# Group 1 of an attention-then-MLP kernel: layer 2 by Strassen's seven block products, with its rows normalised on GpSimd

## The chip, the cores and the metric

The kernel runs on one core of one Trainium2 chip. The core has a matrix engine (TensorE; in the profile PE, and PEld for its weight loads), VectorE (DVE), ScalarE (ACT), GpSimd (POOL), and SyncE (SP), which here issues nearly all DMAs. The metric is device time of one execution, in microseconds; a kernel's time is the median of several executions. Ratios are the mean time of one kernel's fast runs over the mean time of the other's fast runs of the same rounds, so they are not quite the ratio of the medians quoted beside them.

## The reference

```python
# attention: q, k, v of shape (8, 8, 576, 64); causal, window of 64
scores = scale * q @ k.T, masked to 0 <= i - j < 64
attn   = softmax(scores) @ v
x      = attn.transpose(0, 2, 1, 3).reshape(8, 576, 512)
# MLP with a residual
xn  = (x - mean) / sqrt(var + 1e-6) * g_ln
out = x + maximum(xn @ w_ch1, 0) @ w_ch2     # 512 -> 2048 -> 512
```

## The kernel before

The rows are worked off in nine groups of 512: one for the first 512 rows of each of the eight batches, one for all the rest. In every period PE does the MLP of group g in "units" of about 0.87 us, and between the units, at numbered slots, attention steps of the next group are put in. `at(18, b_step, 1, 0)` means: after unit 18, do attention step `b_step` for block 0 of group 1. Where the traces of this case were compared with the program, an engine's instructions stood in its order (in the changed kernel the first z of group 1, whose statistics were ready at 44.3 us, ran on GpSimd at 52.59 us, behind the casts queued before it), so a slot number is read here as setting the order on all engines at once.

A block is 128 rows. `b_step` ends in the block's mean and variance (`mvg`). `z_step` makes the normalised block z, `zt_step` transposes it to zT, the input of layer 1:

```python
def z_step(g, kb):
    ...
    if g < 2:      # groups 0 and 1: VectorE subtracts the mean only, one instruction
        nc.vector.tensor_scalar(out=z, in0=xv, scalar1=mu, scalar2=None, op0=ALU.subtract)
        return
    # groups 2 and on: full normalisation, four dependent GpSimd instructions
    nc.gpsimd.tensor_scalar(out=ve, in0=var, ...)               # var + eps
    nc.gpsimd.tensor_tensor(out=rs, in0=ve, in1=mhalf, op=ALU.pow)
    nc.gpsimd.tensor_scalar(out=nm, in0=mu, scalar1=rs, ...)    # -mean * rs
    nc.gpsimd.tensor_scalar(out=z, in0=xv, scalar1=rs, scalar2=nm, ...)

def zt_step(g, kb, eng="act"):
    if XZ <= g < NGRP - 1 and not (kb == 3 and g in (3, 5)):    # XZ = 2
        nc.sync.dma_start_transpose(out=zT[g][...], in_=z)       # by DMA, SyncE's queue
        return
    ...                                                          # by PE, copied by ScalarE
```

In groups 0 and 1 the scale 1/sqrt(var) is computed later by Newton steps on VectorE and multiplied in after layer 2. Strassen's scheme adds and subtracts blocks of different rows before layer 2, so it needs rows that are fully normalised. Groups 2 and on use it: seven products of half the size in each direction, with four row sums (`s_sums`, VectorE, on the hidden tile hrT) and four sums of blocks of W2 (`w2_sums`, VectorE, once for all groups). Layer 2 of groups 0 and 1 is the plain product: 64 matmuls of 512 columns.

Before the loop over the groups, the program already queues casts on GpSimd, each of which waits for its load:

```python
cast_qk(1, 0); cast_v(1, 0, 1); cast_v(1, 1, 2)
for i in range(8):
    w2_cast(i)                       # W2, in eight pieces
    ...
load_qk(1, 1); load_v(1, 2, 4)
cast_qk(1, 1); cast_v(1, 2, 3); cast_v(1, 3, 4)
# ... here begins the loop over the groups with its slots
```

The softmax here doesn't subtract the row's maximum and nothing guards it: scores larger than these inputs give would overflow.

## Time and profile before

| | before |
|---|---|
| time, first 3 runs | 313.44 and 313.60 us (the third, 504.55, is a slow run and is not used) |
| profiled execution, span | 313.0 us (its time was 314.71 us, 1.2 us above the others) |
| PE busy | 298.9 us, 95% |
| granted TensorE clock, mean | 0.999 |
| group 1: layer 1, layer 2 begin at | 58.75 us, 78.94 us |
| group 2: layer 1 begins at | 96.43 us |

From the page of the kernel before: busy time of the engines, and the granted clock in 40 slices of the span (in tenths; 9 is 90% or more).

```profile
PE 298.9 (95%) x3041; PEld 194.1 (62%) x3041; DVE 205.2 (66%) x385; ACT 153.4 (49%) x258; POOL 166.3 (53%) x251
...
PEclk9999999999999999999999999999999999999999
```

PE is the engine that bounds the kernel (busy for 95% of the span). The timeline of PE around the first two z transposes of group 1 (start, duration, engine, line, operation; in brackets the idle time before and what ended it; xps rows left out):

```profile
46.30 0.39 PE L357 MATMUL ztp<-ident,z 128*128 128x128 f16 x4
47.75 1.46 PE L528 MATMUL ch<-w2s,hrT 128*128 128x512 f16 x6 [1.06 <-POOL w2s L201]
49.04 0.39 PE L357 MATMUL ztp<-ident,z 128*128 128x128 f16 x4
```

PE transposes the first z block at 46.30 us and the second at 49.04 us without waiting: VectorE had written them. The only wait here is for the cast of a piece of W2 (1.06 us). The timeline of GpSimd in the same stretch:

```profile
46.66 1.04 POOL L201 CAST w2s<-w2s 128x1024 f16<-128x1024 f32 x1 [1.27 <-DMA w2s<-in_moe_w_ch_dram]
48.27 1.04 POOL L128 CAST qk<-qk 128x1024 f16<-128x1024 f32 x1 [0.57 <-DMA qk<-in_q_dram]
49.94 1.04 POOL L128 CAST qk<-qk 128x1024 f16<-128x1024 f32 x1 [0.63 <-DMA qk<-in_k_dram]
50.92 1.17 POOL L147 CAST vA<-v 128x512 f16<-128x512 f32 x2
```

The last W2 cast ends at 47.7 us, and the casts of q, k and v of group 1 end at 52.1 us; they wait for their loads. Nobody needs GpSimd for a z of group 1.

Two pieces of the chain that ended last show what a plain and a Strassen matmul cost on PE (start, duration, what):

```profile
79.11 0.86 PE ch L404 x4
...
122.29 1.75 PE pA L464 x16
```

Four plain matmuls take 0.86 us, sixteen of a Strassen product 1.75 us. So 64 plain ones take about 13.8 us and 7 × 16 small ones 12.25 us. The change is after these 1.6 us.

The row of the table of stretches for 78.9 to 96.4 us (busy time and number of instructions of PE, PEld, DVE, ACT and POOL; then PEclk, DMA share, GB/s):

```profile
78.90:96.40 17.50, 17.50 (x178) 8.55 (x176) 10.43 (x21) 4.79 (x7) 11.70 (x22) 1.00 0.67 149
```

### The profile page before, as it was taken

The numbers are of one execution on the slowest core, as the hardware profiler recorded it, in microseconds if no ns is written. First come the engines' busy times: TensorE is split into PE (matmuls) and PEld (weight loads), VectorE is DVE, ScalarE is ACT, GpSimd is POOL, SyncE is SP. The second block draws the span as 40 slices with busy tenths as digits, with TensorE's granted clock in tenths as the row PEclk, the third lists the DMA queues.
The fourth block names the chain that finished last, engine by engine and source line by source line (L and its number), as shares of the span: only waits on it lengthen the run. The fifth ranks groups of instructions, "written<-read, shape, count | busy, mean of one in ns | idle before, by whom it ended". The sixth has DMA issues, their size and how long they took to land.

```text
span 313.0 us, 7473 instructions
## 1 busy us (share of the span) xinstructions
PE 298.9 (95%) x3041; PEld 194.1 (62%) x3041; DVE 205.2 (66%) x385; ACT 153.4 (49%) x258; POOL 166.3 (53%) x251
## 2 busy tenths in 40 slices
PE   6988998899999999999999999999999999999992
PEld 4457544497554468646964686459646855784582
DVE  1689585855674996589666965896669636751642
ACT  1496633477416752776247526762475058306500
POOL 7578666454760798369814983698145506200000
PEclk9999999999999999999999999999999999999999
DMA  8999999998866996798179997993690393003013
GB/s 192 267 390 290 320 336 272 280 304 184 159 144 196 268 206 105 243 312 147 37 212 316 203 149 219 316 142 67 209 172 19 62 209 117 2 2 134 0 36 101
DMA packets 109892, 57.42 MB, mean 183 GB/s; under 512 B 79841, under 2 KB 100833, under 8 KB 109858
## 3 DMA queue, kind: packets, MB, share of 16 engines
q1 hardware_dynamic: 108944, 54.02, 69.1%
q0 software_dynamic: 768, 2.80, 3.7%
q8 instruction: 24, 0.39, 0.5%
q10 hardware_dynamic: 146, 0.13, 0.1%
q14 instruction: 10, 0.08, 0.1%
HBM read 38.80 MB, written 9.44 MB: 154 GB/s over the span
## 4 chain that ended last, share of the span: by engine, by line
PE 74%; DMA 10%; DVE 7%; SPq 4%; POOL 2%; ACT 1%; issue 1%; POOLq 0%; ACTq 0%
PE hps L392 30%; PE pA L464 11%; PE pC L464 7%; PE pB L464 7%; PE ch L404 6%; DMA w2s<-in_moe_w_ch_dram 4%; DMA qk<-in_k_dram 4%; PE xps L317 3%; PE sc L283 3%; PE hph L513 3%; PE tp L226 2%; SPq L141 2%; DVE sS L443 2%; DMA w1s<-in_moe_w_ch_dram 2%; SPq L89 1%; DVE pt L297 1%
## 5 line engine op out<-in xcount | busy, mean ns | idle before, releaser
L392 PE MATMUL hps<-zT,w1g 128*128 128x512 f16 x480 | 110.4, 379 | 0.0
L396 ACT ACTIVATE hrT<-hps 128x512 f16<-128x512 f32 x120 | 71.9, 599 | 50.7 <-PE hps L392 47.2
L392 PEld LDWEIGHTS <-w1g 128*128 128x128 f16 x480 | 44.6, 98 | 49.3 <-issue 1.0
L290 ACT ACTIVATE pt<-sc 128x512 f16<-128x512 f32 x72 | 39.0, 595 | 29.8 <-DVE xn L471 15.6
L464 PEld LDWEIGHTS <-sS 128*128 128x128 f16 x448 | 43.3, 98 | 5.1
L342 POOL TENSOR_SCALAR rsz<-mvg 128x1 f32<-128x1 f32 x28 | 10.7, 382 | 60.4 <-DVE mvg L328 59.8
L128 POOL CAST qk<-qk 128x1024 f16<-128x1024 f32 x32 | 35.1, 1112 | 13.4 <-DMA qk<-in_q_dram 6.9
L464 PEld LDWEIGHTS <-hrT 128*128 128x128 f16 x336 | 32.6, 98 | 5.2
L212 ACT COPY qkT<-tp 128x1024 f16<-128x1024 f16 x16 | 16.1, 1012 | 35.2 <-PE tp L226 26.1
L297 DVE TENSOR_TENSOR pt<-pt,mask 128x1024 f16<-128x1024 f16 x32 | 25.4, 800 | 11.9 <-ACT pt L290 11.9
L471 DVE TENSOR_TENSOR xn<-pA,xn 128x512 f32<-128x512 f32 x28 | 19.2, 686 | 21.1 <-PE pA L464 21.1
L443 DVE TENSOR_TENSOR sS<-hrT 128x512 f16<-128x512 f16 (+1 forms) x42 | 24.8, 591 | 10.2 <-ACT hrT L396 10.2
L464 PE MATMUL pA<-wT,sS 128*128 128x256 f16 x224 | 26.9, 273 | 0.0
L345 POOL TENSOR_SCALAR z<-xn,rsz 128x512 f16<-128x512 f32 x28 | 25.3, 902 | 2.9
L464 PE MATMUL pC<-w2s,sS 128*128 128x256 f16 x224 | 26.8, 273 | 0.0
L325 DVE BATCH_NORM_STATS2 stats<-xn 128x6 f32<-128x512 f32 x36 | 25.0, 695 | 1.2
L323 DVE TENSOR_TENSOR xn<-xps,rcp 128x512 f32<-128x512 f32 x36 | 24.9, 692 | 1.2
L513 PE MATMUL hph<-zT,w1g 128*128 128x256 f16 x192 | 23.2, 272 | 2.3 <-ACT zT L360 1.1
L320 DVE RECIPROCAL rcp<-xps 128x8 f32<-128x8 f32 x36 | 7.4, 205 | 26.8 <-PE xps L317 26.8
L404 PE MATMUL ch<-w2s,hrT 128*128 128x512 f16 x96 | 23.1, 380 | 0.0
L513 PEld LDWEIGHTS <-w1g 128*128 128x128 f16 x192 | 18.3, 98 | 5.1 <-issue 2.6
L317 PEld LDWEIGHTS <-pt 128*64 128x64 f16 x576 | 12.2, 110 | 14.4 <-issue 6.4
(85 smaller groups left out, 395.1 us busy)
## 6 DMA issues: line engine op xcount, KB each, us to landing
out_dram<-xn SPq DMA_DIRECT2D x34, 256.0 KB, 2.6
qk<-in_q_dram SPq DMA_DIRECT2D x16, 512.0 KB, 6.2
qk<-in_k_dram SPq DMA_DIRECT2D x16, 512.0 KB, 7.4
v<-in_v_dram SPq DMA_DIRECT2D x32, 256.0 KB, 6.5
w2s<-in_moe_w_ch_dram SPq DMA_DIRECT2D x12, 512.0 KB, 5.7
w1s<-in_moe_w_ch_dram SPq DMA_DIRECT2D x4, 512.0 KB, 6.7
tk<-in_k_dram SPq DMA_DIRECT2D x8, 256.0 KB, 4.7
tv<-in_v_dram SPq DMA_DIRECT2D x8, 256.0 KB, 5.3
```

The costliest lines, as they stand in the source:

```text
L128: nc.gpsimd.tensor_copy(out=dst[:, :].rearrange("p (a j) e d -> p a e j d", j=j), in_=t[:, :].rearrange("p (a e j d) -> p a e j d", e=2, j ...
L290: nc.scalar.activation(out=o, in_=i, func=AF.Exp, bias=0.0, scale=scale)
L297: nc.vector.tensor_tensor(out=ptv, in0=ptv, in1=mb, op=ALU.mult)
L323: nc.vector.tensor_tensor(out=xn, in0=xps[:, :, 0:D], in1=rcp_b, op=ALU.mult)
L325: nc.vector.bn_stats(out=stats, in_=xv)
L345: nc.gpsimd.tensor_scalar(out=z, in0=xv, scalar1=rs, scalar2=nm, op0=ALU.mult, op1=ALU.add)
L392: nc.tensor.matmul(out=hps, lhsT=w1g[:, kc, 128 * hc:128 * (hc + 1)], rhs=zT[g][:, kc, :], start=(kc == 0), stop=(kc == NKC - 1),)
L396: nc.scalar.activation(out=hrT[:, hc, :], in_=hps, func=AF.Relu, bias=0.0, scale=1.0)
L404: nc.tensor.matmul(out=ch[kb], lhsT=hrT[:, hc, 128 * kb:128 * (kb + 1)], rhs=w2s[:, hc, :], start=(hc == 0), stop=(hc == NHC - 1),)
L443: nc.vector.tensor_tensor(out=o, in0=x, in1=y, op=op)
L464: nc.tensor.matmul(out=bank[which][:, p, :], lhsT=a[:, c, 128 * p:128 * p + 128], rhs=wv[:, c, :], start=(first and p == 0 and c == 0), st ...
L513: nc.tensor.matmul(out=hps[:, e], lhsT=w1g[:, kc, 128 * hc:128 * (hc + 1)], rhs=zT[g][:, kc, 256 * half:256 * half + 256], start=(kc == 0) ...
```

## The change

The intent: layer 2 of group 1 by seven products as well. For that its z is fully normalised, on GpSimd like those of later groups, the Newton steps of group 1 go, the W2 sums move to period 0 and the start of period 1, and some slots move because group 1 has 30 units in place of 32. The diff, cut to its core:

```diff
-        if g < 2:                      # in b_step
+        if g == 0:
             z_step(g, kb)
-        if g < 2:                      # in z_step: subtract on VectorE, or all on GpSimd
+        if g == 0:
-            if g < 2:                  # in add_out: scale after layer 2
+            if g == 0:
-        units, s_sums = mlp_units(g, (8, 16)[g] if g < 2 else 0, g == 0, g > 1)
+        units, s_sums = mlp_units(g, (8, 16)[g] if g < 2 else 0, g == 0, g > 0)
 ... period 0
             at(18, b_step, 1, 0)
+            at(18, z_step, 1, 0)
             at(21, b_step, 1, 1)
-            at(22, zt_step, 1, 0)
-            at(24, zt_step, 1, 1)
+            at(21, z_step, 1, 1)
+            at(23, zt_step, 1, 0)
+            at(27, zt_step, 1, 1)
+            for m, i in enumerate((3, 2, 4)):
+                at(25 + 2 * m, w2_sums, i, 0, 4)
+                at(26 + 2 * m, w2_sums, i, 4, 8)
 ... 
+            at(31, z_step, 1, 2)
 ... period 1
-            at(0, cast_qk, 2, 1)
+            at(2, cast_qk, 2, 1)
-            at(2, zt_step, 1, 2)
-            at(13, newton, 1, 0, 4)
-            at(5, zt_step, 1, 3)
+            at(1, z_step, 1, 3)
+            at(2, w2_sums, 1, 0, 4)
+            at(3, w2_sums, 1, 4, 8)
+            at(3, zt_step, 1, 2)
+            at(7, zt_step, 1, 3)
+            for i in range(1, 5):
+                at((12, 12, 13, 14)[i - 1], s_sums, 0, 4, i)
+                at((16, 16, 18, 20)[i - 1], s_sums, 4, 8, i)
 ... (W2 sums leave periods 1 and 2; slots of group 3's steps; order of two buffers)
```

More of the change, by code (lines that the diff above doesn't have):

```diff
@@ L303, in b_step @@
             if (g, kb // 2) not in x_norm:
-                for h in ((1, 0) if g // 2 == 2 else (0, 1)):
+                for h in ((1, 0) if g in (3, 4, 7) else (0, 1)):
                     x_norm[(g, h)] = p_xn.tile([128, 2, DM], FP32, tag="xn" + sfx, name=f"xn_{g}_{h}", bufs=nb)
@@ L719 @@
             at(6, t_main, 2, 1, 1)
-            at(25, w2_sums, 3, 0, 4)
-            at(28, w2_sums, 3, 4, 8)
             for j in range(4):
@@ L738 @@
             at(17, make_vB, 3)
-            at(31, s_mm, 3, 0)
-            at(31, s_mask, 3, 0)
-            for i, (x, half) in zip((12, 24, 12, 28), ((0, 0), (1, 0), (0, 1), (1, 1))):
+            at(28, s_mm, 3, 0)
+            at(29, s_mask, 3, 0)
+            for i, (x, half) in zip((12, 22, 12, 25), ((0, 0), (1, 0), (0, 1), (1, 1))):
                 at(i, t_main, 3, x, half, 0)
@@ L745 @@
             at(40, load_v, 4, 0, 4)
-        if g == 2:
-            for m, i in enumerate((2, 1, 4)):
-                at(4 + 2 * m, w2_sums, i, 0, 4)
-                at(5 + 2 * m, w2_sums, i, 4, 8)
         if g > 1 and g + 2 < B:
@@ L807 @@
         for i, u in enumerate(units):
-            if g > 1 and i == 20:
+            if g > 0 and i == 20:
                 tbank["shared"] = True
```

## The prediction

> **What bounds the kernel now.** PE: the totals give 298.9 us busy of 313.0 (95%), clock 0.999; after 79 us the wait view shows PE idle for only 0.3 us before a matmul. So a stage lasts for PE's work plus PE's waits. In the timeline, group 1 runs from 58.75 to 96.4 us: 20.2 us of layer 1 (PE busy 18.4; it waits 0.74 us for the relu, 0.44 for an addition of group 0, 0.64 for VectorE's Newton steps), then layer 2.
>
> **What the change removes.** Layer 2 of group 1 is 64 matmuls of 512 columns; the chain shows 4 in 0.865 us: 13.8 us. The seven products are 112 of 256 columns, 16 in 1.75 us in later groups: 12.25 us. Gain 1.6 us. The Newton steps go (0.64 us). The W2 sums leave groups 1 and 2: 0.3 us at most. Together about 2.5 us if nothing new waits.
>
> **What it adds.** Four blocks on GpSimd, each a chain of four operations of 2.1 to 2.5 us together (first block of group 2: 78.93 to 81.34). VectorE wrote the same z in 0.49 us. VectorE gets eight W2 sums of 0.68 us and eight row sums of 0.70.
>
> **Where it hurts: queue order on GpSimd.** [...] this trace's order agrees wherever I compared it with the program. Before the loop the program queues the W2 casts and the q/k and v casts of group 1. In the timeline they wait for their loads: last W2 cast done at 47.7 us, q/k casts at 49.3 and 51.0, last v cast at 52.1. No z was behind them; now the first z of group 1 is, so it is done at about 54.4 us and the second at 56.8, although their statistics are there at 44.5 and 47.5. PE wants the first transpose after unit 23, at 48.6 us (that unit waits for W2 until 47.75), and stops: about 5.8 us.
>
> Afterwards VectorE is late too: its W2 sums come behind an addition that waits for PE, and its chain to the statistics of the third block runs without a pause to about 67 us. Group 1 starts at about 65.2 (before: 58.75). Then GpSimd does z, two casts, z, two casts (9 us) up to 76; the q/k transposes of group 2 wait for it, about 1.5 us, and PE waits 0.6 us for the last zT copy. The second half of layer 1 starts at about 78.4, before 69.85: +8.5. Minus Newton, layer 2 and group 2's relief: +6.
>
> **Prediction.** 319.0 us, 80% range 315.0 to 322.5. Faster by over 2%: 0.02; within 2%: 0.55; slower by over 2%: 0.43 (the line is at 319.9).
>
> **What would show it.** Right: one PE wait of 5 to 6 us at a transpose of group 1's z, released by GpSimd, between 48 and 55 us; group 1 beginning at 64 to 66 us; a PE wait of 1 to 2 us for a q/k cast around 75 us; layer 2 of group 1 shorter by 1.6 us; later periods as long as before, so the loss stays. Wrong: z of group 1 running among the W2 casts, or PE without a gap near 50 us.
>
> **What would make it wrong.** If GpSimd's queue is not in the order in which I read the program, the stall vanishes: 311 to 313 us. If the later waits overlap more, the loss is the first stall less the gain: 316 to 317. GpSimd slowed by VectorE's two-input sums would make it 321 or more.

The forecast's sum stays at about +5.5 us, 319.0 us. What is said of the queue order rests on the order in the trace of the kernel before and on the times given there. That VectorE's sums would slow GpSimd, and the 321 us, were a supposition and an estimate; what the runs show of it is the second z chain on GpSimd, 3.6 us beside W2 sums in e1 and 2.6 us with these sums moved away in e8.

## The result, and the profile after

The changed kernel takes 328.11 us (327.63 to 328.58, four runs), against 313.47 us (three fast runs): the ratio is 1.0466, with a 95% interval of 1.0445 to 1.0486. It is 14.6 us slower, where the prediction said 5.5. The profiled execution spans 326.5 us.

From the page of the changed kernel, the two lines shown of before:

```profile
PE 300.6 (92%) x3089; PEld 199.3 (61%) x3089; DVE 209.1 (64%) x381; ACT 153.7 (47%) x258; POOL 171.4 (52%) x267
...
PEclk9999996999999799999999999999999999999998
```

PE is busy for about as long as before, in a span 13.5 us longer, and its clock now drops in three slices (to 6, 7 and 8 tenths). PE's waits (engine, line, what it waited for: us in total, times, longest), three of the largest:

```profile
PE ztp L357 <- POOL z L345: 6.3, 1, 6.3
...
PE hps L392 <- DMA zT<-z: 2.3, 1, 2.3
PE xps L317 <- DVE pt L297: 1.9, 3, 0.9
```

The first is one wait of 6.3 us for a z on GpSimd. GpSimd's timeline shows why:

```profile
46.27 1.04 POOL L201 CAST w2s<-w2s 128x1024 f16<-128x1024 f32 x1 [0.81 <-DMA w2s<-in_moe_w_ch_dram]
48.20 1.04 POOL L128 CAST qk<-qk 128x1024 f16<-128x1024 f32 x1 [0.89 <-DMA qk<-in_q_dram]
50.35 1.04 POOL L128 CAST qk<-qk 128x1024 f16<-128x1024 f32 x1 [1.11 <-DMA qk<-in_k_dram]
51.33 1.17 POOL L147 CAST vA<-v 128x512 f16<-128x512 f32 x2
52.59 0.19 POOL L342 TENSOR_SCALAR rsz<-mvg 128x1 f32<-128x1 f32 x1
52.87 0.56 POOL L343 TENSOR_TENSOR rsz<-rsz,mhalf 128x1 f32<-128x1 f32 x1
53.52 0.27 POOL L344 TENSOR_SCALAR rsz<-mvg,rsz 128x1 f32<-128x1 f32 x1
53.89 0.76 POOL L345 TENSOR_SCALAR z<-xn,rsz 128x512 f16<-128x512 f32 x1
```

The casts stand as before, up to 52.5 us. Then the four instructions of the first z of group 1 follow at once (52.59 to 54.65 us), although its statistics had been ready on VectorE since 44.3 us. PE's timeline:

```profile
47.37 1.02 PE L528 MATMUL ch<-w2s,hrT 128*128 128x512 f16 x4 [0.83 <-POOL w2s L201]
54.71 0.61 PE L357 MATMUL ztp<-ident,z 128*128 128x128 f16 x4 [6.33 <-POOL z L345]
55.12 1.06 PE L528 MATMUL ch<-w2s,hrT 128*128 128x512 f16 x2
55.97 2.76 PE L404 MATMUL ch<-w2s,hrT 128*128 128x512 f16 x8
```

PE had nothing to do from 48.4 to 54.7 us. After the wait its matmuls are slow: eight plain ones take 2.76 us, where they take 1.89 us in e1 and e2 below. The table of stretches shows the same: each row is a stretch, with the busy time (and number of instructions) of PE, PEld, DVE, ACT and POOL, then PEclk, DMA share and GB/s. The last two stretches belong to the start of group 2:

```profile
48.40:54.70 6.30, 0.00 (x0) 0.00 (x0) 0.35 (x1) 0.00 (x0) 4.77 (x8) 0.70 0.88 261
54.70:58.40 3.70, 3.69 (x14) 1.68 (x15) 2.19 (x4) 0.58 (x1) 1.77 (x4) 0.59 1.00 345
88.70:106.70 18.00, 16.31 (x226) 13.22 (x224) 15.79 (x30) 5.68 (x9) 12.85 (x22) 1.00 0.49 95
106.70:109.10 2.40, 0.05 (x2) 0.03 (x1) 1.29 (x2) 0.19 (x1) 0.00 (x0) 0.96 0.88 262
109.10:113.50 4.40, 4.40 (x20) 1.57 (x22) 0.00 (x0) 1.23 (x3) 0.00 (x0) 0.63 1.02 312
```

The granted clock is 0.70 in the wait, 0.59 in the 3.7 us behind it (0.50 from 51.5 to 57.7 us, the "half clock" of the expectations below), and 0.63 in the 4.4 us that follow a second wait, the one of 2.3 us for `DMA zT<-z`. That second wait nobody had foreseen. SyncE's timeline around it:

```profile
105.31 0.83 SPq L430 DMA_DIRECT2D out_dram<-xn  x2
106.24 1.21 SPq L353 DMA_TRANSPOSE zT<-z  x1
```

GpSimd finished the last z of group 2 at 104.37 us, but SyncE issued its transpose (L353) only at 106.24 us: behind two output stores of group 1 (L430), which waited for VectorE's last product sums. It landed too late for PE:

```profile
105.70 1.05 PE L464 MATMUL pC<-w2s,sS 128*128 128x256 f16 x8
109.10 4.33 PE L392 MATMUL hps<-zT,w1g 128*128 128x512 f16 x12 [2.35 <-DMA zT<-z]
```

In the kernel before, the same twelve matmuls began at 96.43 us and took 2.81 us:

```profile
96.43 2.81 PE L392 MATMUL hps<-zT,w1g 128*128 128x512 f16 x12
```

The differences add up along PE, from the starts in the two timelines. (The spans differ by 13.5 us and the times by 14.6, because the profiled execution of the kernel before was a longer one.) "Layer 2" runs from the first matmul of group 1's layer 2 to the last before group 2.

| stretch | predicted | measured |
|---|---|---|
| wait at the first z transpose | +5.8 | +6.3 |
| low clock after it (54.71 to 58.56 us: 3.85 us; 2.39 in run e2 below, where the clock stays up) | none | +1.5 |
| rest of period 0 | +0.65 | +0.2 |
| layer 1 of group 1, Newton wait gone (22.00 us against 20.19) | +1.4 | +1.8 |
| layer 2 of group 1 without the wait behind it (18.0 against 17.5) | −1.6 | +0.5 |
| wait for zT of group 2 | none | +2.35 |
| low clock after it (12 matmuls in 4.33 us against 2.81) | none | +1.5 |
| later (what is left of the span) | −0.3 | −0.7 |
| sum | +6 | +13.5 |

So the forecast of the sum missed 7.5 us: 3.85 at the border to group 2, 2.1 in layer 2, 1.5 of low clock after the first wait; the other rows nearly cancel.

### The profile page after: what moved, and what is told of

Its sections match the earlier page's. It is cut to its first block, busy times and chain, and to the rows that moved or that the text cites. A ratio compares the mean times of both kernels' runs of the same rounds, so it can differ in the third digit from the quotient of the medians.

```text
span 326.5 us, 7585 instructions
## 1 busy us (share of the span) xinstructions
PE 300.6 (92%) x3089; PEld 199.3 (61%) x3089; DVE 209.1 (64%) x381; ACT 153.7 (47%) x258; POOL 171.4 (52%) x267
## 4 chain that ended last, share of the span: by engine, by line
PE 68%; DMA 15%; SPq 6%; POOL 4%; DVE 4%; issue 1%; POOLq 0%
PE hps L392 31%; PE pA L464 12%; PE pB L464 8%; PE pC L464 8%; DMA qk<-in_k_dram 7%; DMA v<-in_v_dram 4%; SPq L141 3%; PE xps L317 3%; PE sc L283 2%; DMA w2s<-in_moe_w_ch_dram 2%; POOL qk L128 2%; PE tp L226 2%; DMA w1s<-in_moe_w_ch_dram 2%; SPq L89 1%; PE ch L404 1%
## 5 line engine op out<-in xcount | busy, mean ns | idle before, releaser
L392 PE MATMUL hps<-zT,w1g 128*128 128x512 f16 x480 | 111.9, 383 | 2.3 <-DMA zT<-z 2.3
L464 PEld LDWEIGHTS <-sS 128*128 128x128 f16 x512 | 49.3, 98 | 5.9
L464 PEld LDWEIGHTS <-hrT 128*128 128x128 f16 x384 | 37.1, 98 | 5.8
L471 DVE TENSOR_TENSOR xn<-pA,xn 128x512 f32<-128x512 f32 x32 | 21.9, 686 | 21.5 <-PE pA L464 21.5
L297 DVE TENSOR_TENSOR pt<-pt,mask 128x1024 f16<-128x1024 f16 x32 | 27.8, 873 | 10.9 <-ACT pt L290 10.8
L443 DVE TENSOR_TENSOR sS<-hrT 128x512 f16<-128x512 f16 (+1 forms) x46 | 27.5, 599 | 10.2 <-ACT hrT L396 10.2
L212 ACT COPY qkT<-tp 128x1024 f16<-128x1024 f16 x16 | 16.1, 1012 | 36.3 <-PE tp L226 32.0
L464 PE MATMUL pA<-wT,sS 128*128 128x256 f16 x256 | 30.9, 273 | 0.1
L464 PE MATMUL pC<-w2s,sS 128*128 128x256 f16 x256 | 30.9, 273 | 0.0
L345 POOL TENSOR_SCALAR z<-xn,rsz 128x512 f16<-128x512 f32 x32 | 28.2, 880 | 3.4 <-POOL rsz L344 0.2
L343 POOL TENSOR_TENSOR rsz<-rsz,mhalf 128x1 f32<-128x1 f32 x32 | 22.3, 696 | 2.7
```

The costliest lines, as they stand in the source:

```text
L297: nc.vector.tensor_tensor(out=ptv, in0=ptv, in1=mb, op=ALU.mult)
L392: nc.tensor.matmul(out=hps, lhsT=w1g[:, kc, 128 * hc:128 * (hc + 1)], rhs=zT[g][:, kc, :], start=(kc == 0), stop=(kc == NKC - 1),)
L443: nc.vector.tensor_tensor(out=o, in0=x, in1=y, op=op)
L464: nc.tensor.matmul(out=bank[which][:, p, :], lhsT=a[:, c, 128 * p:128 * p + 128], rhs=wv[:, c, :], start=(first and p == 0 and c == 0), st ...
```

## The experiments

Theory A is the prediction's: z stands behind casts in GpSimd's queue. Rival B: VectorE, which was given W2 sums and row sums, makes PE late. Fourteen kernels ran (there is no e7), four of them with wrong numbers on purpose (e5, e6, e14, e15). "e4 + ..." means an edit on top of e4. Times are medians of fast runs; "before" was run in the same rounds and took 313.5 to 314.6 us. Rounds ran on different chips, so runs of different rounds are best compared by their ratios.

| run | what it is | time, us | ratio to before, 95% interval |
|---|---|---|---|
| changed kernel | | 328.11 | 1.0466 (1.0445 to 1.0486) |
| e1_late_zt | two z transposes later on PE | 322.12 | 1.0258 (1.0217 to 1.0300) |
| e2_dummy | PE kept busy in the wait | 326.44 | 1.0403 (1.0344 to 1.0463) |
| e3_zt26 | zT of group 2 ahead of the stores | 324.88 | 1.0363 (1.0330 to 1.0396) |
| e4_both | e1 and e3 | 318.54 | 1.0129 (1.0078 to 1.0180) |
| e5_dve_z | z back on VectorE, wrong numbers | 319.41 | 1.0174 (1.0141 to 1.0208) |
| e6_dve_z26 | e5 and e3, wrong numbers | 316.40 | 1.0067 (1.0009 to 1.0125) |
| e8_sums_g1 | e4 + W2 sums in group 1 | 318.51 | 1.0121 (1.0084 to 1.0157) |
| e9_z_alone | before + z on GpSimd | 324.35 | 1.0302 (1.0260 to 1.0343) |
| e10_order | e4 + work of group 1 reordered | 318.72 | 1.0168 (1.0134 to 1.0202) |
| e11_new | e10 + two z on VectorE, sums moved | 317.60 | 1.0124 (1.0095 to 1.0153) |
| e12_tuned | e11 + its waits mended | 317.96 | 1.0145 (1.0114 to 1.0176) |
| e13_no_seven | e12 with plain layer 2 | 317.38 | 1.0124 (1.0093 to 1.0156) |
| e14_no_row_sums | e6 without row sums, wrong numbers | 315.95 | 1.0057 (1.0031 to 1.0083) |
| e15_no_sums | e14 without early W2 sums, wrong numbers | 314.74 | 1.0023 (0.9998 to 1.0048) |

### z on GpSimd alone (e9_z_alone)

```diff
 # on the kernel before
-        if g < 2:     # in b_step, z_step and add_out
+        if g == 0:
-            at(22, zt_step, 1, 0); at(24, zt_step, 1, 1)
+            at(18, z_step, 1, 0); at(21, z_step, 1, 1)
+            at(23, zt_step, 1, 0); at(27, zt_step, 1, 1)   # Newton gone; no products, no sums
```

> The kernel before with only the z of group 1 moved to GpSimd (fully normalised, Newton steps gone, transposes and casts at the changed kernel's places); layer 2 as before, no sums moved. Theory A (queue order on GpSimd): the 6 us wait and the half clock are all there without any Strassen part, and group 1's first half is late by about 2 us: 321 to 323.5. Rival B (sums and products are the cost): within 1.5 us of before.

It took 324.35 us, 3.0% over before: about 9.5 us, slightly more than expected. PE's waits in this run:

```profile
PE ztp L357 <- POOL z L345: 6.2, 1, 6.2
```

The same wait, without any Strassen part in the kernel. Rival B cannot explain this run: the z on GpSimd alone brings 3.0 of the 4.66%, two thirds of the loss.

### Only PE's order changed (e1_late_zt)

```diff
-            at(23, zt_step, 1, 0)
-            at(27, zt_step, 1, 1)
+            at(30, zt_step, 1, 0)
+            at(31, zt_step, 1, 1)
```

> The changed kernel; only the two PE transposes of group 1's first z blocks stand later in PE's order (after units 30 and 31 instead of 23 and 27). GpSimd's order and all work are the same. Theory A (PE stops at a transpose whose z stands behind casts in GpSimd's queue): the 6.3 us wait and the half clock behind it go, group 1 starts near 60 instead of 66.7 us, time 319.5 to 321.5. Rival B (VectorE, given the W2 sums and row sums, is what makes PE late): the wait only moves to VectorE's results, time above 325.

322.12 us, so 6.0 us of 14.6 (6.5 by the ratios) came back from an edit that moves eight small matmuls on PE, and with them ScalarE's two copies of their results, and leaves the order on GpSimd and VectorE as it was. That is what theory A says, though 0.6 us outside its range, and less than the 7.8 us of wait and slow clock together. The rest is in a new wait of 2.0 us at the second transpose. PE's and GpSimd's timelines of this run:

```profile
59.34 0.40 PE L357 MATMUL ztp<-ident,z 128*128 128x128 f16 x4 [2.02 <-POOL z L345]
```

```profile
55.65 0.24 POOL L342 TENSOR_SCALAR rsz<-mvg 128x1 f32<-128x1 f32 x1
55.97 1.01 POOL L343 TENSOR_TENSOR rsz<-rsz,mhalf 128x1 f32<-128x1 f32 x1
57.07 1.35 POOL L344 TENSOR_SCALAR rsz<-mvg,rsz 128x1 f32<-128x1 f32 x1
58.52 0.76 POOL L345 TENSOR_SCALAR z<-xn,rsz 128x512 f16<-128x512 f32 x1
```

The second z chain took 3.6 us (55.65 to 59.28), against 2.05 us in the changed kernel (54.74 to 56.79). In the changed kernel VectorE was idle for most of that time (until 56.22 us), because it waited for PE; in e1 it was doing W2 sums and mask products. For one column per partition (L344) 0.27 us became 1.35 us; the instruction ended at 58.42 us, right after a row of four instructions with two inputs on VectorE (two W2 sums and two mask products, 55.87 to 58.37). What happens without the W2 sums there is tested in e8.

### PE kept busy in the wait (e2_dummy)

```diff
+            at(23, keep_clock_t, 24)     # 24 matmuls of 512 columns into a buffer of the transposes
             at(23, zt_step, 1, 0)
```

> The changed kernel with 24 idle-filling matmuls of 512 columns (about 5.2 us) on PE ahead of the first transpose of group 1's z; the wait for GpSimd stays, only PE isn't idle in it. If the idle PE loses clock and the matmuls after it run slower for it, the granted clock stays at 1.0 between 48 and 60 us and the time falls by 1 to 2 us, to 326 to 327. If the slow matmuls there have another cause, the time stays at 328.1 or rises.

326.44 us: 1.7 us less, with 24 useless matmuls more. Its interval overlaps that of the changed kernel (1.0344 to 1.0463 against 1.0445 to 1.0486), so the time alone does not settle it; the profile is clearer. PE's timeline:

```profile
47.67 5.34 PE L603 MATMUL warmt<-mbias,ident 128*128 128x512 f16 x24
53.93 0.40 PE L357 MATMUL ztp<-ident,z 128*128 128x128 f16 x4 [0.92 <-POOL z L345]
...
54.60 1.89 PE L404 MATMUL ch<-w2s,hrT 128*128 128x512 f16 x8
```

Eight plain matmuls after the wait take 1.89 us again. The row for 54.7 to 58.4 us of the table of stretches has a clock of 1.00 (0.59 in the changed kernel):

```profile
54.70:58.40 3.70, 3.69 (x32) 2.15 (x30) 2.96 (x4) 1.61 (x3) 1.11 (x3) 1.00 0.88 302
```

So the idle PE, not the wait as such, cost the extra 1.5 us. The profiled execution is the fastest of the four (324.35 us), but part of its lead has another source: it has the second wait too (2.4 us for the zT of group 2), but its mean clock is 0.997, against 0.990 in e1, whose profile has a low clock behind the second wait alone. The same wait in the changed kernel (2.35 us) and in e1 (2.3 us) was followed by a clock of 0.63 and 0.64 in the next 4.4 and 4.2 us. Whether a wait of this length costs clock therefore differs between executions: the mean clocks of e2's four are 0.997, 0.996, 0.992 and 0.987, at 324.35, 325.48, 327.39 and 328.49 us. Two more waits in profiles: behind 2.02 us in e1 the clock was 1.00 (59.3 to 64.0 us), behind 2.92 us in e12 it was 0.57 (90.5 to 94.5 us). From what length on a wait costs clock is not shown here.

### The transpose of group 2 ahead of the stores (e3_zt26), and both edits (e4_both)

```diff
-                at((18, 21, 24, 27)[j], zt_step, 2, j)
+                at((18, 21, 24, 26)[j], zt_step, 2, j)
```

> The changed kernel with the transpose of group 2's last z block issued one unit earlier (after unit 26, not 27), so that it stands before the two output stores of group 1 in SyncE's queue. Theory A (these stores wait for the last product sums of VectorE and hold the transpose back by 1.9 us, then PE waits 2.35 us for it and runs its next 4 us at a low clock): PE's wait at group 2's first matmul falls below 0.5 us, the clock stays, time 323.5 to 325. Rival B (the z itself comes too late from VectorE and GpSimd): wait still 1.5 us or more, time 327 to 328.

324.88 us, 3.2 us less. In PE's timeline the wait is 0.3 us, and the twelve matmuls take 2.78 us (clock 1.00 from 106.5 to 111.0 us):

```profile
106.50 2.78 PE L392 MATMUL hps<-zT,w1g 128*128 128x512 f16 x12 [0.32 <-DMA zT<-z]
```

The z was in time; its place in SyncE's queue was not. This wait's own rival B (the z comes too late) falls.

> Both moves together: group 1's first two z transposes late in PE's order, group 2's last z transpose ahead of the stores. If the two losses are independent (6.0 us and 3.2 us measured apart), 318.5 to 319.5 us. If they are one loss seen twice, not below 321.

318.54 us: in ratios, 0.0208 and 0.0103 measured apart, 0.0337 together. Within the intervals the two losses add up, as independent ones do.

### Products and sums with z on VectorE (e5_dve_z, e6_dve_z26)

```diff
     def z_step(g, kb):
-        if g == 0:
+        if g < 2:      # subtract the mean on VectorE; the products then mix unscaled rows: wrong numbers
```

> The changed kernel, but group 1's z is written by VectorE as before (mean subtracted, not scaled): wrong numbers in group 1 on purpose. Seven products, W2 sums and row sums stay as in the change. Theory A (the z on GpSimd is the cost): no wait for GpSimd at group 1's transposes, time 316 to 319.5, of which about 4 us are the late zT of group 2, which stays. Rival B (VectorE's added sums are the cost): VectorE now has even more to do, time 325 or more.

319.41 us over its three fast runs, at the upper end of what theory A expects; rival B's 325 is excluded. Its profile fell in a slow execution (385.4 us, clock 0.756) and its waits are not read.

> Group 1's z on VectorE again (wrong numbers in group 1 on purpose) with group 2's last z transpose ahead of the stores: the seven products, W2 sums and row sums alone. The forecast's account (a gain of 2.5 us if nothing new waits) expects 311 to 312.5. If the sums on VectorE make PE wait in group 1's second half by themselves, 314.5 to 317, with PE waiting for VectorE's mask product before the attention matmuls of group 2.

316.40 us, 0.7% over before: the first expectation, a gain of 2.5 us, was wrong, the second (314.5 to 317) right. This run has neither the queue wait nor the late zT, and still loses 2 us. With e9 (+3.0%) and the zT of group 2 (+1.0%, from the changed kernel against e3) it closes the account: 3.0 + 1.0 + 0.7 = 4.7% of the 4.66% measured. That it closes so well is partly luck: the three intervals together leave about 0.8 either way, and the Newton steps are gone in both e9 and e6. PE waits for VectorE's mask products, twice in layer 2 (0.80 and 0.55 us) and once before it (0.42):

```profile
PE xps L317 <- DVE pt L297: 1.8, 3, 0.8
```

### W2 sums elsewhere (e8_sums_g1)

```diff
 # on e4
-            for m, i in enumerate((3, 2, 4)):            # period 0
-                at(25 + 2 * m, w2_sums, i, 0, 4); at(26 + 2 * m, w2_sums, i, 4, 8)
+            for m, i in enumerate((3, 2, 4, 1)):         # period 1, after units 7 to 11
+                at((7, 8, 9, 11)[m], w2_sums, i, 0, 4); at((7, 8, 9, 11)[m], w2_sums, i, 4, 8)
```

> As e4_both, with all eight W2 sums taken out of period 0 and done in group 1 after units 7 to 11, where VectorE idles. In e1 the second z chain on GpSimd took 3.6 us beside the W2 sums, against 2.1 us in the changed kernel without them. If VectorE's two-input sums hold GpSimd up, both chains are near 2.1 us again, PE's 2.0 us wait at the second transpose falls below 0.7, and time is 1 to 2 us under e4_both. If GpSimd's length has another cause (loads), wait and time stay, or rise by the sums' new place.

GpSimd's chains were 2.3 and 2.6 us and PE's wait 1.0 us, so most of the extra length came from the W2 sums, though the wait did not fall below the expected 0.7. But the time stayed at 318.51 us: the sums met other GpSimd work in the new place, and PE's waits for mask products grew from 1.9 us (e4) to 5.0. VectorE's and GpSimd's timelines:

```profile
72.55 5.31 DVE L561 TENSOR_TENSOR wT<-wT,w2s 128x1024 f16<-128x1024 f16 x2
```

```profile
73.33 3.98 POOL L128 CAST qk<-qk 128x1024 f16<-128x1024 f32 x4
```

Two sums that take 1.3 us took 5.31 us. They ended at 77.86 us, 0.55 us after the last of four casts in a row (73.33 to 77.31 us). The changed kernel has the same at its first mask product of group 2: 2.82 us (83.37 to 86.19) in place of 0.69, beside four casts (81.65 to 85.63); it too ended about 0.55 us after the last cast.

### Attempts at a better version (e10 to e13)

```diff
 # e10, on e4: row sums as late as their products allow; two casts of group 3 later
-                at((12, 12, 13, 14)[i - 1], s_sums, 0, 4, i); at((16, 16, 18, 20)[i - 1], s_sums, 4, 8, i)
+                at((12, 15, 19, 22)[i - 1], s_sums, 0, 4, i); at((16, 18, 20, 24)[i - 1], s_sums, 4, 8, i)
-            at(8, cast_qk, 3, 0); at(10, cast_qk, 3, 1)
+            at(8, cast_qk, 3, 0, (0,)); at(10, cast_qk, 3, 1, (0,)); at(17, cast_qk, 3, 0, (1,)); at(20, cast_qk, 3, 1, (1,))
-            at(7, zt_step, 1, 3)
+            at(5, zt_step, 1, 3)
 # e11, on e10: Newton for two columns, then z = (x - mean) * rstd on VectorE for blocks 0 and 1
+        if g == 1 and kb < 2:
+            nc.vector.tensor_scalar(out=z, in0=xv, scalar1=mu, scalar2=rstd[1][:, kb:kb + 1],
+                                    op0=ALU.subtract, op1=ALU.mult)
 #      casts of group 2 queued before GpSimd's z of blocks 2 and 3; all W2 sums after units 3 to 11 of group 1
```

> e4_both with the work of group 1 reordered, none added: each row sum on VectorE as late as its product allows instead of ahead of the mask products, two of the four casts of group 3's q/k moved from beside the first mask (which took 2.8 us there instead of 0.7) to later, and the last zT of group 1 two units earlier. If PE's remaining waits in group 1 (0.45, 0.92 and 0.55 us for masks, 0.94 for zT) come from that order, most of them go: 315 to 317 us, against 318.5. If VectorE is simply full there, they come back at other places: 318 or more.

> e10_order, and group 1's first two blocks normalised on VectorE (Newton steps for two columns, then one subtract-and-scale of about 0.5 us each, after unit 24) instead of GpSimd; group 2's q/k casts ahead of the other two z on GpSimd; all W2 sums in group 1 after units 3 to 11. No z stands behind a cast that waits for a load. If the queue order was the whole loss, 311.5 to 314, level with before or just better; if the seven products cannot pay at all here because VectorE has no room for their sums, 315 to 318.

In both the hopeful branch missed and the other held. e10 took 318.72 us: the waits for masks went and came back as waits for group 3's casts (0.86 and 0.95 us, from my own move), for a row sum (0.70) and for the vB copy (1.35). e11 has no z behind a cast in group 1's first two blocks, and took 317.60 us.

```diff
 # e12, on e11
-            at(27, t_main, 1, 1, 1, 1)                    # copy on VectorE
+            at(27, t_main, 1, 1, 1, 0)                    # copy on ScalarE
 #      group 3's late casts at slots 14 and 17, one row sum at 17 instead of 18, attention block 3 at 22 instead of 23
 # e13, on e12: layer 2 of group 1 plain, its row sums gone, W2 sums where they were before
```

> e11_new with its own new waits mended, no work added: in period 0 ScalarE, not VectorE, copies the q/k transpose that stood behind the Newton steps (1.04 us of PE wait), group 3's two late casts stand two to three units before PE wants them (0.86 and 0.95 us), one row sum a unit earlier (0.63), the last attention block of group 2 a unit earlier. If each wait was PE's own delay, about 3.5 us less than e11_new: 313 to 314.5, that is level with before. If VectorE's room is the limit, the waits reappear elsewhere: 315.5 or more.

> e12_tuned with layer 2 of group 1 as before (64 matmuls of 512 columns) and without its row sums; the W2 sums at the places they have in the kernel before. What is left of the change is its preparation alone. If the seven products are worth their 1.6 us of PE work once nothing waits, this is 1 to 2 us slower than e12_tuned; if VectorE's work eats it, equal or faster.

e12 did not gain on e11: 317.96 us. The mended waits are gone, and new ones are in their place, a large one above all. PE's timeline:

```profile
90.55 0.22 PE L317 MATMUL xps<-vB,pt 128*64 128x65 f16 x1 [2.92 <-DVE pt L297]
...
93.59 2.17 PE L468 MATMUL pA<-wT,sS 128*128 128x256 f16 x16
```

The step that I had put one unit earlier now came before its mask product, which VectorE finished late. 2.92 us of wait, a clock of 0.57 in the 4 us behind it, and still sixteen matmuls in 2.17 us instead of 1.91. e13, without the seven products, took 317.38 us, the same within the error: in this arrangement the products earn nothing. It also says that what e12 loses against before is not the price of the products: the preparation alone is 1.2% slower, and PE never waits there for a z on GpSimd. Which part of it costs that was not tested. No version that I ran beats the kernel before.

### Where the gain of the products goes (e14_no_row_sums, e15_no_sums)

```diff
 # e14, on e6: no s_sums in group 1; its products read parts of hrT in place of the row sums
 # e15, on e14: no W2 sums in periods 0 and 1 either; its products read W2 in place of the W2 sums
```

> e6_dve_z26 (z on VectorE, wrong numbers in group 1 on purpose) without group 1's eight row sums: its products read parts of the hidden tile instead, equally many matmuls of equal size. e6 took 2 us more than before, where the forecast's gain of 2.5 us was to be. If the row sums on VectorE eat the gain, the waits for mask products in layer 2 go and the time is 313 to 314.5 (0.993 to 1.002 of before); if they are harmless, 1.005 or more.

> e14_no_row_sums without W2 sums in period 0 and group 1 either (all eight in group 2; products of group 1 read W2 itself; wrong numbers in group 1 on purpose). What is left is the PE side of the change with no added VectorE work. If the forecast of 1.6 us from layer 2 and 0.6 from the Newton steps holds where nothing waits: 0.990 to 0.996 of before. If PE's own time for seven products is not shorter, 1.0 or more.

By the tests as they were set, both hopes failed: e14 (1.0057) fell in the branch "harmless", e15 (1.0023) in "1.0 or more". The profiles by stretch say something else about layer 2 (starts on PE, in us; the wait for group 2's zT is taken off layer 2):

| | layer 1 of group 1 | layer 2 of group 1 |
|---|---|---|
| before | 20.2 (58.75 to 78.94) | 17.5 |
| e6: products, row sums, W2 sums | 21.1 (58.63 to 79.75) | 17.8 |
| e14: products, W2 sums | 21.5 (59.02 to 80.56) | 16.1 |
| e15: products alone | 20.1 (59.90 to 80.00) | 16.1 |

PE does save its time: layer 2 is 1.4 us shorter in e14 and e15, close to the 1.6 us forecast. Layer 2 in e14 and then in e15, PE's timelines:

```profile
80.56 1.04 PE L466 MATMUL pA<-w2s,hrT 128*128 128x256 f16 x8
...
97.15 2.79 PE L392 MATMUL hps<-zT,w1g 128*128 128x512 f16 x12 [0.51 <-DMA zT<-z]
```

```profile
80.00 1.04 PE L467 MATMUL pA<-w2s,hrT 128*128 128x256 f16 x8
...
95.03 1.05 PE L467 MATMUL pC<-w2s,hrT 128*128 128x256 f16 x8
96.60 2.79 PE L392 MATMUL hps<-zT,w1g 128*128 128x512 f16 x12 [0.52 <-DMA zT<-z]
```

With the row sums on VectorE (e6) these 1.4 us are gone: layer 2 takes 17.8 us, 1.35 of them in two waits for mask products that e14 does not have. A cost of the W2 sums is not shown: layer 1 is 1.4 us longer in e14 than in e15, but that is one wait of 1.40 us for an addition of group 0, and e15 has such a wait already in period 0 (0.94 us), so that over both stages it is 0.6 us ahead; the times (1.0057 and 1.0023, same rounds) differ by no more than their error. The step from e6 to e14 is not resolved in the times (1.0067 and 1.0057, from different rounds), although layer 2 is 1.7 us shorter in the profile; one profile each is thin evidence for a microsecond. And even e15 is no faster than before: its profile has a wait of 0.94 us for the last zT copy of group 1 and 0.52 us for the zT of group 2, both at steps whose slots the change moved, and one of 0.94 us for an addition on VectorE in period 0, for which I have no cause.

## Why the prediction was right or wrong

**Right: the main mechanism.** PE waits at the first z transpose of group 1, released by GpSimd, for 6.3 us (said: about 5.8, between 48 and 55 us). The reason is the order of the queue: z's statistics were there at 44.3 us, its first instruction ran at 52.59, right behind the last cast. e1 moved only PE's order and got 6.0 us back; e9 has the wait without Strassen.

**Right: the knock-on in group 1.** The q/k transposes of group 2 waited 0.67 and 0.36 us (said: 1.5; the profile puts the first to ScalarE, whose result came 0.03 us after the cast) and PE waited 0.94 us for the zT copy (said: 0.6).

**Wrong: "Group 1 starts at about 65.2".** It was 66.72 us. Left out was the granted clock: after 6.3 us without work PE ran at 0.50 from 54.7 to 57.7 us. This cost 1.5 us here and 1.5 us after the second wait; e2 shows it for the first, e3 for the second. After the long wait the matmuls were slow in e9 too (eight plain ones in 3.62 us behind 6.24 us of wait); after a wait of 2.4 us the low clock can stay away, as in e2 (mean clock 0.997).

**Wrong: "Minus Newton, layer 2 and group 2's relief: +6".** Of the 7.5 us by which the sum was missed, 2.1 are here. The forecast took 1.6 us of PE work as 1.6 us of time. VectorE was busy for 10.4 of 17.5 us in layer 2 before (in 78.9 to 96.4 us) and for 15.8 of 18.0 us after. The mask products of the next group stand between the new sums in its queue, and PE waited for three of them (1.9 us in all, 1.5 us of it in layer 2). Layer 2 became 0.5 us longer, not 1.6 shorter; e14's profile has the saving once the row sums are away, but its time does not show it, so this cause rests on one profile each. The prediction had costed the row sums (0.70 us each) and then left them out of layer 2; it counted the W2 sums only on the way to the third block's statistics.

**Wrong: "later periods as long as before, so the loss stays".** This is the step that failed most: 3.85 of the 7.5 us. The border to group 2 was not looked at. With two units less in group 1, the last z transpose of group 2 stood one place behind stores that wait for the very last product sums: 2.35 us of wait and 1.5 us of low clock. e3 takes both away by moving one number.

**What stays open.** Whether a schedule exists in which the seven products pay in group 1, and why the preparation alone (e13) costs 1.2%. Five attempts (e4, e8, e10, e11, e12) ended 1.2 to 1.7% over before. How much of VectorE's lateness is its amount of work, and how much is GpSimd's work beside it (two W2 sums took 5.31 us beside four casts in e8, 1.3 us otherwise), was not taken apart.

## What to carry to other kernels

Before giving an engine new work, read what already stands ahead of it in that engine's queue, above all instructions that wait for loads (6.3 us of wait here), and check every queue at both borders of the changed stage, the DMA-issuing one included (2.35 us here). Where the bounding engine is TensorE, count a long wait as more than its idle time, since the clock can be low behind it (here 0.59 in the 3.7 us behind 6.3 us, 1.5 us lost). A saving on the bounding engine is only worth something if the engine that pays for it (here VectorE) has room in the same stretch, in the place in its queue where others wait for it (layer 2 took 16.1 us in e14 without the row sums, 17.8 us in e6 with them).
